# A long convolution with a SwiGLU FFN on one core: taps loaded as rows, the first inverse with a negated basis, another order

## Chip, cores and metric

The kernel runs on one core of a Trainium2 chip. The metric is the device time of one execution in microseconds (us), taken as the median of the runs. Beside it there is one profiled execution, whose trace is read here. Engines are named as the profile names them: PE is TensorE, DVE is VectorE, ACT is ScalarE, POOL is GpSimd, and SP is the engine that issues most DMAs. A label such as L695 is a line of the kernel before.

## The reference, cut to what matters

With S = 2048 rows and D = 640 channels:

```
k_shift = sum over t of pad(k)[:, t:t+S] * shift_k[:, 3-t]     # four taps
kv      = k_shift * v
y       = irfft(rfft(kv, 2S) * rfft(ssm_k, 2S))[:, :S] + kv * ssm_D
h       = x + layernorm(x) * y
out     = h + (silu(n @ w_gate) * (n @ w_up)) @ w_down,  n = layernorm(h)
```

F, the width of the FFN, is 1728. Everything is bf16 in memory.

## The kernel before

The sequence is cut into four blocks of 512 rows; a tile has 128 partitions with four rows r each. Block by block the kernel makes the product kv, its spectrum X, the spectrum G of that block of the filter, the sum of the products of spectra over all earlier blocks, the inverse transform, the gated residual h, the second norm and the FFN.

**Taps (L498 to L506, L885).** The shift convolution is done on PE: `diag` (L885) holds the four taps of each channel on small diagonals, 32 channels wide, and 140 matmuls per block (L504) work on 32-row strips of the transposed k. `tapw`, 128 x 5 x 4, holds the taps channel by channel; it is read straight from memory by L874, where four taps of a channel are 8 bytes in a row. DVE builds `diag` from `tapw` and a folded identity (L882, L883).

**Spectra (`transform`, L324; matmuls L308; evictions L297 on ACT or L300 on DVE).** A spectrum of 512 frequencies is held in two halves. By symmetry the second half needs only another sign of the odd rows, so in the plain form ("sub") the odd part is evicted twice over and DVE subtracts (L343). In the form "four" DVE has six operations in place of that one (L360, L364, L367), and PE half of the matmuls. In the form with `minus`, a second basis that is the negated and scaled one, PE accumulates the second half itself, with six matmuls in place of four per quarter, and DVE has nothing to do. Block 0 works in two pieces of 320 channels (`SPLIT`). G0 takes `minus`; X0 does not.

**Products (`mac`, L531; L538 for the first term, L564 and L565 for the others).** All on DVE.

**Inverse (`inverse`, L646; matmuls L695).** In the plain form DVE first makes the difference and the sum of the two halves (L656, L659), and PE uses four matmuls per row and piece. With `minus` there is no DVE work and there are eight matmuls per row and piece. Then the first norm is applied (L637), the result is multiplied with the inverse (L707), and added to x (L713); ACT sums squares (L577); the small steps of the norm are L590 to L612 on DVE; the second norm is applied by L637 on DVE or L640 on ACT; `turn_h` transposes h on PE (L733) or by DMA and ACT or DVE evict it (L735).

**FFN (`ffn`, L754).** L775 and L810 are gate and up, 512 columns per matmul; L792 is the silu, L799 and L801 the product, or L798 straight from PSUM; L842 is the down projection, 320 columns per matmul; L847 and L848 add the result to the output in memory, and in the last block L857 and L859 with a store by SP (L861).

**The order.** Each step is recorded as a numbered operation with its engine, its reads and its writes (`Plan.add`). `Plan.run` emits them in the order of the table `ORDER`. A negative entry -n stands for operation n - 1 on the other engine that it offers: an eviction that is on ACT goes to DVE, and the product L799 with L801 becomes the one L798. Buffers come from pools of fixed size (`SLOTS`), handed out when an operation first touches them: four PSUM tiles `ps`, twelve large tiles `big`, five `row` tiles. Engines work in their program order, so the table also sets which wait blocks what. On SP, loads that must wait for a buffer hold up the loads behind them.

`DIRECT` names the spectra and the inverse that take `minus`; `SUM` names those that take "four". `ACTLN` and `ACTLN2` say from or in which blocks a norm is offered to ACT. X0 and G0 are given no name at L903 and L904, so that `SUM` isn't looked up for them.

Of the kernel before, what the change touches and what calls it, by code (L numbers as in the profile page):

```python
# [11 lines left out]
BF16 = mybir.dt.bfloat16  # L12
# [7 lines left out]
P = 128  # L20
# [6 lines left out]
KT = D // P  # L27
# [5 lines left out]
ADDLO, ADDMAC, ADDWIN, ADDH, LEAD = (), (), (), (2,), {}  # L33
PAD = 16
WARM = 24
DIRECT, ACTLN, ACTKV, ACTLN2 = ('G0',), 1, 1, (2, 3)
LN1DVE, LN2POOL, HTURN = (0, 1, 2, 3), (), (2, 1)
GTURN = (3, 1, 2)
SUM = {'i3': 'four', 'G1': 'four', 'X1': 'four', 'X0': 'four'}
ADDP = {}  # L40
K0TURN = False
SLOTS = {"S": 8, "big": 12, "kT": 2, "tT": 1, "row": 5, "sg": 2, "ps": 4, "sm": 6}
ORDER = (
# [44 lines left out]
SPLIT = ((0,), (1,))  # L88
ROWS = (1, 3, 0, 2)
HALVES = (ROWS[:2], ROWS[2:])  # L90
# [81 lines left out]
def kernel(ctx: ExitStack, tc: tile.TileContext, A_q, A_k, A_v, A_shift_k, A_ssm_k, A_ssm_D, B_x,  # L172
          B_w_gate, B_w_up, B_w_down, out):
    nc = tc.nc
# [20 lines left out]
    def new(kind):  # L195
        return Buf(views.get(kind, (kind,))[0], kind)

    def fixed(shp, dt, name):
        return Buf(None, None, const.tile(shp, dt, name=name))

    def ap(b):
        if b.pool is None:
            return b.ap
        t = place[b.pool][b.at]
        _, how, sizes = views.get(b.kind, (None, None, None))
        return t.rearrange(how, **sizes) if how else t

    def pe(ns, fn, r, w):
        return plan.add("pe", ns, fn, r, w)
# [12 lines left out]
    def load(nbytes, fn, w, r=()):  # L222
        return plan.add("sp", nbytes / 300.0, fn, r, w)
# [23 lines left out]
    ident = fixed([P, P], BF16, "ident")  # L247
    WF = fixed([P, R, 4, P], BF16, "WF")
    WI = fixed([P, 4, R, P], BF16, "WI")
    tapw = fixed([P, KT, 4], BF16, "tapw")  # L250
    diag = fixed([P, KT * 4, ROWT], BF16, "diag")
    eye = fixed([P, 2 * ROWT], BF16, "eye")
    wd = fixed([P, NCH, D], BF16, "wd")
# [144 lines left out]
    def turned(b):  # L398
        return ap(b).rearrange("p a b -> p (a b)").bitcast(BF16)
# [24 lines left out]
    def spectrum(src, pieces=((0, 1),), minus=None, name=None):  # L424
        b = new("S")
        transform(src, b, pieces, minus, name)
        return Spec(b)
# [443 lines left out]
            nc.gpsimd.memset(t[64:P, NC_FULL, :], 0.0)  # L871
    plan.add("pool", 2000, blank, [], [blanks])
    k = load_k(0)
    load(1e3, lambda: nc.sync.dma_start(out=ap(tapw), in_=A_shift_k.rearrange("(c p) t -> p c t", p=P)), [tapw])  # L874
    idle = new("ps")

    def warm():
        for _ in range(WARM):
            nc.tensor.matmul(ap(idle)[:, 0, 0:P], ap(ident), ap(ident), start=True, stop=True)
    pe(110 * WARM, warm, [ident], [idle])  # L880
    def fold():
        nc.vector.tensor_add(ap(eye), ap(ident)[:, 0:2 * ROWT], ap(ident)[:, 2 * ROWT:P])  # L882
        nc.vector.tensor_add(ap(eye)[:, 0:ROWT], ap(eye)[:, 0:ROWT], ap(eye)[:, ROWT:2 * ROWT])  # L883
# [8 lines left out]
    minus = new("tT")  # L892
# [7 lines left out]
        k = turned_k(k)  # L900
    kv = kv_of(0, k, None, v)
    gT = g_turned(g, drow)
    X = [spectrum(kv, SPLIT, minus if "X0" in DIRECT else None)]  # L903
    G = [spectrum(gT, SPLIT, minus if "G0" in DIRECT else None)]  # L904
    H = [G[0]]
    n1 = ln1(x)
    A = Spec(new("S"))
# [77 lines left out]
```

## Time and profile before

| | us |
|---|---|
| median of three runs | 265.37 |
| lowest and highest | 264.68, 266.27 |
| the profiled execution, its own time | 265.86 |
| its span in the trace | 263.8 |
| PE busy in the span | 247.7 |
| DVE busy | 209.3 |
| ACT busy | 173.4 |
| POOL busy | 22.1 |

The page cuts the span into 40 slices of 6.6 us and gives the busy share of each engine in tenths, with the TensorE clock granted in the row PEclk. A timeline line has start, length, engine, line, operation, tiles and count, and in brackets the idle time before it with what ended it. A line of the waits has who waited for whom, the total in us, the number of times and the longest.

### The profile page before, as it was taken

The page shows a single profiled execution, that of the slowest core. Times are in us where ns is not written, and L with a number is a line of the kernel's source. Part 1 is how long each engine was busy: PE and PEld are TensorE (multiplying, and loading weights), DVE is VectorE, ACT ScalarE, POOL GpSimd, SP SyncE. Part 2 cuts the span into 40 slices and gives each one's busy share as a digit, 9 for nine tenths or more (in the row PEclk, how much of TensorE's full clock was granted, in tenths as well). Part 3 has the DMA queues.
Part 4 walks back from the last instruction along what each step waited for, and adds up shares of the span by engine and source line. Part 5 has one row for each costly group of instructions (what it writes and reads, how often), then busy time and mean ns, then how long its engine had stood idle before and what let it go on. Part 6 is the DMA issues. An engine that isn't in the chain of part 4 may idle for free. (4 is left out here: it accounts for less than half of the span.)

```text
span 263.8 us, 5064 instructions
## 1 busy us (share of the span) xinstructions
PE 247.7 (94%) x2004; PEld 146.1 (55%) x2004; DVE 209.3 (79%) x326; ACT 173.4 (66%) x296; POOL 22.1 (8%) x26
## 2 busy tenths in 40 slices
PE   3989596999999999999999999999999999999995
PEld 3866363544555777754445667544447774444673
DVE  2589989989999999899999999999999831122122
ACT  3799979999888959653538886359743871462200
POOL 2001700000000004010001300220000004000000
PEclk9999779999999999999999999999999999999999
DMA  6889499994687857999389634867999007000011
GB/s 169 311 276 276 110 191 222 316 255 66 159 303 249 143 115 132 116 230 244 93 197 235 98 102 88 162 133 183 283 262 261 3 2 99 0 0 2 0 50 50
DMA packets 73880, 40.81 MB, mean 155 GB/s; under 512 B 34113, under 2 KB 71810, under 8 KB 73858
## 3 DMA queue, kind: packets, MB, share of 16 engines
q1 hardware_dynamic: 71554, 37.88, 56.6%
q0 software_dynamic: 2304, 2.62, 7.7%
q8 instruction: 15, 0.25, 0.4%
q14 instruction: 7, 0.06, 0.1%
HBM read 30.01 MB, written 4.59 MB: 131 GB/s over the span
## 5 line engine op out<-in xcount | busy, mean ns | idle before, releaser
L775 PE MATMUL ps<-big,big 128*128 128x512 bf16 x480 | 106.2, 379 | 0.8 <-ACT sg L792 0.6
L775 PEld LDWEIGHTS <-big 128*128 128x128 bf16 x480 | 46.8, 98 | 56.8 <-issue 1.4
L842 PE MATMUL ps<-wd,tT 128*128 128x320 bf16 x448 | 62.8, 299 | 0.0
L842 PEld LDWEIGHTS <-tT 128*128 128x128 bf16 x448 | 43.8, 98 | 17.3
L792 ACT ACTIVATE sg<-ps 128x1024 bf16<-128x1024 f32 (+1 forms) x28 | 27.0, 965 | 35.5 <-PE ps L775 13.7
L308 PE MATMUL ps<-big,WF 128*128 128x320 bf16 x224 | 35.1, 302 | 3.0 <-ACT S L297 2.1
L564 DVE TENSOR_TENSOR big<-S,S 128x2560 bf16<-128x2560 bf16 x24 | 35.3, 1479 | 0.0
L565 DVE TENSOR_TENSOR S<-S,big 128x2560 bf16<-128x2560 bf16 x24 | 35.2, 1479 | 0.0
L308 PEld LDWEIGHTS <-WF 128*128 128x128 bf16 x224 | 22.0, 99 | 14.0 <-issue 3.7
L799 ACT CAST sg<-ps 128x1024 bf16<-128x1024 f32 (+1 forms) x26 | 24.6, 948 | 4.8 <-PE ps L775 4.5
L801 DVE TENSOR_TENSOR tT<-sg,sg 128x1024 bf16<-128x1024 bf16 (+1 forms) x26 | 16.7, 642 | 10.7 <-ACT sg L799 10.7
L577 ACT ACTIVATE row<-big 128x640 bf16<-128x640 bf16 x32 | 23.5, 738 | 2.0 <-DVE big L713 1.9
L848 POOL DMA_DIRECT2D out_dram<-row x12 | 10.7, 1136 | 144.3 <-ACT row L847 136.3
L297 ACT CAST S<-ps 128x320 bf16<-128x320 f32 (+1 forms) x39 | 19.3, 544 | 4.1 <-PE ps L308 3.9
L640 ACT ACTIVATE row<-big,sm 128x640 bf16<-128x640 bf16 x18 | 15.7, 923 | 4.9 <-DVE sm L590 4.9
L695 PEld LDWEIGHTS <-WI 128*128 128x128 bf16 x112 | 11.6, 104 | 9.8 <-issue 3.9
L810 PE MATMUL ps<-big,big 128*128 128x512 bf16 x60 | 14.4, 379 | 0.0
L297 ACT ACTIVATE big<-ps 128x640 bf16<-128x640 f32 (+1 forms) x23 | 13.6, 636 | 1.2 <-PE ps L308 1.0
L707 DVE SCALAR_TENSOR_TENSOR row<-row,ps 128x640 bf16<-128x640 bf16 x16 | 12.9, 814 | 0.9 <-PE ps L695 0.5
L629 ACT ACTIVATE row<-big 128x640 bf16<-128x640 bf16 x16 | 11.7, 736 | 2.0 <-DMA big<-in_A_q_dram 2.0
L538 DVE TENSOR_TENSOR S<-S,S 128x2560 bf16<-128x2560 bf16 (+1 forms) x10 | 12.1, 1215 | 0.0
L538 DVE TENSOR_TENSOR big<-S,S 128x2560 bf16<-128x2560 bf16 (+1 forms) x10 | 12.1, 1215 | 0.0
(78 smaller groups left out, 233.0 us busy)
## 6 DMA issues: line engine op xcount, KB each, us to landing
big<-in_B_w_up_dram SPq DMA_DIRECT2D x24, 320.0 KB, 4.5
big<-in_B_w_gate_dram SPq DMA_DIRECT2D x24, 320.0 KB, 3.9
big<-in_A_q_dram SPq DMA_DIRECT2D x4, 640.0 KB, 6.3
big<-in_A_v_dram SPq DMA_DIRECT2D x4, 640.0 KB, 4.4
big<-in_A_ssm_k_dram SPq DMA_DIRECT2D x4, 640.0 KB, 7.0
wd<-in_B_w_down_dram SPq DMA_DIRECT2D x1, 2080.0 KB, 10.7
out_dram<-big SPq DMA_DIRECT2D x3, 640.0 KB, 5.4
out_dram<-row POOLq DMA_DIRECT2D x12, 160.0 KB, 4.6
```

The costliest lines, as they stand in the source:

```text
L297: (lambda: nc.scalar.activation(dst(), src(), ACT.Copy, scale=2.0)) if twice else (lambda: nc.scalar.copy(dst(), src())),
L308: nc.tensor.matmul(ap(ps)[:, h, 0:NH], w, ap(src)[:, r, h * NH:(h + 1) * NH], start=(first and i == 0), stop=(last and i == len(rs) - 1), ...
L538: return lambda: f(*(x() for x in args))
L564: dve(1490, lambda b=b, xs=xs, hs=hs: nc.vector.tensor_mul(flat2(b), X.part(xs), H.part(hs)), [X.at(xs), H.at(hs)], [b])
L565: dve(1490, lambda b=b, dst=dst, f=f: f(A.part(dst), A.part(dst), flat2(b)), [b], [A.at(dst)])
L577: act(930, lambda r=r, junk=junk: nc.scalar.activation(ap(junk), ap(x)[:, r, :], ACT.Square, scale=D ** -0.5, accum_out=sm(s, 1)[:, r:r + ...
L640: nc.scalar.activation(ap(row), ap(x)[:, r, :], ACT.Identity, bias=sm(s, 5)[:, r:r + 1], scale=sm(s, 4)[:, r:r + 1])
L775: nc.tensor.matmul(of(ps, i), ap(w)[:, k, off:off + P], ap(hT)[:, k, lo:lo + n], start=(k == 0), stop=(k == KT - 1))
L792: act(1010 if wide else 600, lambda: nc.scalar.activation(of(sg), of(*gate), ACT.Silu), [gate[0]] if gate[0] is up[0] else [(gate[0], gate ...
L799: op = plan.add("act", 1010 if wide else 590, lambda: nc.scalar.copy(of(co), of(*up)), psu + [sg], [co] + tt, ("dve", 1230 if wide else 69 ...
L801: op.rest = dve(690 if wide else 420, lambda: nc.vector.tensor_mul(to(), of(sg), of(co)), [sg, co], tt)
L842: nc.tensor.matmul(ap(to)[:, hf, 0:NH], ap(tT)[:, c, at:at + P], ap(wd)[:, c, hf * NH:(hf + 1) * NH], start=(c == order[0]), stop=(c == or ...
```

## The change

The taps are loaded as five rows of 128 channels by four taps (1 KB each), into a new tile `tap5` on five partitions. PE transposes them, one transpose of 128 x 5 per tap, and one eviction writes `tapw`. The load stands between the two halves of the first k. The inverse of block 0 takes `minus`. The table `ORDER` is another one, with the numbers of the operations moved by two. `ACTLN` and `ACTLN2` now offer more norm steps to ACT, and the table takes the other engine for some; X0 and G0 get their names, and `SUM` loses X0.

```diff
-DIRECT, ACTLN, ACTKV, ACTLN2 = ('G0',), 1, 1, (2, 3)
+DIRECT, ACTLN, ACTKV, ACTLN2 = ('G0', 'inv0'), 0, 1, (0, 1, 2, 3)
-SUM = {'i3': 'four', 'G1': 'four', 'X1': 'four', 'X0': 'four'}
+SUM = {'i3': 'four', 'G1': 'four', 'X1': 'four'}
 ORDER = (
...
+    tap5 = fixed([KT, P * 4], BF16, "tap5")
...
-    load(1e3, lambda: nc.sync.dma_start(out=ap(tapw), in_=A_shift_k.rearrange("(c p) t -> p c t", p=P)), [tapw])
+    load(1e3, lambda: nc.sync.dma_start(out=ap(tap5), in_=A_shift_k.rearrange("(c p) t -> c (p t)", p=P)), [tap5])
...
+    pt = new("ps")
+
+    def turn_taps(pt=pt):
+        for t in range(4):
+            nc.tensor.transpose(turned(pt)[:, t * 8:t * 8 + KT], ap(tap5).rearrange("c (p t) -> c t p", t=4)[:, t, :], ap(ident)[0:KT, 0:KT])
+    pe(240, turn_taps, [tap5, ident], [pt])
+    evict(lambda copy, pt=pt: copy(ap(tapw).rearrange("p c t -> p t c"), turned(pt)[:, 0:32].rearrange("p (t c) -> p t c", c=8)[:, :, 0:KT]),
+          [pt], [tapw], ns=200, other=140)
...
-    X = [spectrum(kv, SPLIT, minus if "X0" in DIRECT else None)]
-    G = [spectrum(gT, SPLIT, minus if "G0" in DIRECT else None)]
+    X = [spectrum(kv, SPLIT, minus if "X0" in DIRECT else None, "X0")]
+    G = [spectrum(gT, SPLIT, minus if "G0" in DIRECT else None, "G0")]
```

Counted over the built programs, PE gains 32 matmuls of L695 and the four transposes. DVE loses two L656 and two L659 of 320 columns by four rows and one eviction of the transposed k, and gains three evictions of spectra (two of 320 columns and one of 640) and one of h. ACT loses those and gains the eviction of k and that of the taps. All other groups keep their counts on each engine.

88 rows, old and new, of the table ORDER are left out of this document.

## The prediction

> **What bounds the kernel now.** I read the page first, for the share of each engine and for the stretches in which the busiest one is not busy.
>
> ```profile
> PE 247.7 (94%) x2004; PEld 146.1 (55%) x2004; DVE 209.3 (79%) x326; ACT 173.4 (66%) x296; POOL 22.1 (8%) x26
> PE   3989596999999999999999999999999999999995
> DVE  2589989989999999899999999999999831122122
> PEclk9999779999999999999999999999999999999999
> ```
>
> TensorE (PE) is the bound over the whole span, and VectorE (DVE) runs beside it without a hole up to the thirtieth slice, about 198 us. So two chains are nearly equally late. Only the front is loose: slices 5 to 8 of the PE row hold 5, 9, 6, and in two of them the granted clock is 0.7. The waits of PE say what ended those holes:
>
> ```profile
> PE ps L695 <- ACT big L524: 2.9, 1, 2.9
> PE ps L308 <- ACT S L297: 2.1, 4, 0.9
> ```
>
> The timeline of PE places them, and gives the point at which the first FFN begins:
>
> ```profile
> 14.90 4.55 PE L308 MATMUL ps<-big,WF 128*128 128x320 bf16 x32 [0.71 <-ACT big L393]
> 26.19 1.43 PE L504 MATMUL ps<-diag,kT 32*128 32x128 bf16 x140
> 30.50 1.23 PE L695 MATMUL ps<-big,WI 128*128 128x320 bf16 x4 [2.88 <-ACT big L524]
> 34.04 2.34 PE L695 MATMUL ps<-S,WI 128*128 128x320 bf16 x8
> 48.22 4.49 PE L775 MATMUL ps<-big,big 128*128 128x512 bf16 x20
> ```
>
> And the chain that ended last gives the rest (start, length, what):
>
> ```profile
> 142.89 1.42 DVE big L528
> 168.64 6.47 PE ps L775 x30
> 197.77 5.43 PE ps L842 x40
> 260.67 0.49 DVE row L859
> ```
>
> From 144.3 us, when DVE finishes the product L528 of the last block, the chain is PE alone up to the last DVE addition. Its rates are prices: 6.47/30 = 0.216 us for a 512-wide matmul, 5.43/40 = 0.136 for a 320-wide one. In the instruction order of the two built programs the PE work from the first L775 on is equal in both: 540 of 512, 648 of 320 columns and the same small ones, 208.7 us at these rates. So the change is worth what it moves the first L775 (48.22) and the L528 of the last block (144.3), plus new waits behind them.
>
> **The taps.** Three windows of 1 us and two for the clock (the last columns are granted clock, DMA share, GB/s):
>
> ```profile
> 4.00:5.00 1.00, 1.00 (x11) 1.00 (x11) 0.36 (x1) 0.00 (x0) 0.00 (x0) 1.00 0.98 101
> 5.00:6.00 1.00, 1.00 (x12) 0.93 (x9) 0.48 (x4) 0.83 (x2) 0.00 (x0) 1.00 0.97 215
> 8.00:9.00 1.00, 1.00 (x63) 0.88 (x52) 0.00 (x0) 0.59 (x1) 0.00 (x0) 1.00 1.01 391
> 29.00:30.00 1.00, 0.00 (x0) 0.00 (x0) 1.00 (x2) 1.00 (x3) 1.00 (x1) 0.78 0.00 0
> 36.00:37.00 1.00, 1.00 (x8) 0.64 (x7) 0.58 (x1) 0.24 (x1) 0.00 (x0) 0.81 1.32 291
> ```
>
> Between 4 and 6 us the DMA engines are fully busy and move 101 and 215 GB/s, against 391 later: this is where 640 runs of 8 bytes pass. Five rows of 1 KB should give back at most (1 - 101/391) + (1 - 215/391) = 1.2 us to whatever stands behind them in the queue, at least nothing. Behind them stand x and v, and both are waited for:
>
> ```profile
> 5.92 0.82 DVE L885 TENSOR_TENSOR diag<-eye,tapw 128x640 bf16<-128x640 bf16 x1 [0.49 <-DMA tapw<-in_A_shift_k_dram]
> 10.11 2.48 DVE L526 TENSOR_TENSOR big<-ps,big 128x512 bf16<-128x512 f32 x4 [2.96 <-DMA big<-in_A_v_dram]
> 20.60 0.82 DVE L538 TENSOR_TENSOR big<-S,S 128x1280 bf16<-128x1280 bf16 x1
> 25.76 0.81 DVE L656 TENSOR_TENSOR big<-S 128x1280 bf16<-128x1280 bf16 x1
> 26.49 0.82 DVE L538 TENSOR_TENSOR S<-S,S 128x1280 bf16<-128x1280 bf16 x1
> 31.82 1.55 DVE L659 TENSOR_TENSOR S<-S 128x1280 bf16<-128x1280 bf16 x2
> 39.67 0.81 DVE L707 SCALAR_TENSOR_TENSOR row<-row,ps 128x640 bf16<-128x640 bf16 x1
> 44.14 1.51 DVE L637 TENSOR_SCALAR row<-big,sm 128x640 bf16<-128x640 bf16 x4
> 201.38 1.56 DVE L673 TENSOR_TENSOR S<-S 128x1280 bf16<-128x1280 bf16 x2
> ```
>
> ScalarE (ACT), which sits in the turn of G0 and in the eviction of every spectrum, shows the same wait for x and then hardly any:
>
> ```profile
> 8.41 0.74 ACT L629 ACTIVATE row<-big 128x640 bf16<-128x640 bf16 x1 [1.95 <-DMA big<-in_A_q_dram]
> 23.15 3.62 ACT L297 CAST S<-ps 128x320 bf16<-128x320 f32 x10 [0.16 <-PE ps L308]
> 29.09 2.61 ACT L524 CAST big<-ps 128x512 bf16<-128x512 f32 x6
> 31.52 2.59 ACT L378 COPY big<-big 128x2560 bf16<-128x2560 bf16 x1
> 36.76 1.29 ACT L297 CAST S<-ps 128x640 bf16<-128x640 f32 x2 [1.44 <-PE ps L308]
> 41.25 0.76 ACT L577 ACTIVATE row<-big 128x640 bf16<-128x640 bf16 x1
> 46.78 1.29 ACT L735 COPY big<-ps 128x640 bf16<-128x640 bf16 x2
> ```
>
> Against this gain: diag now waits for four transposes of 5 columns and a small copy. No row shows such a copy; it lies between nothing and the 0.65 us of one of the L524 or kT copies (1.29 for two in the L735 row), and I take 0.3, as it moves 20 of 640 columns. It stands on ACT behind two kT copies, so diag starts near 6.1 instead of 5.92 and the last kT copy, now behind diag on DVE, ends about 0.3 later than before. The kT transposes and taps on PE run that much later, under the wait for v (10.11), then the warm-up block, the rest of the taps and the turn of G0 follow without a hole. So the spectra (L308) start at about 14.2 instead of 14.90: PE's own queue keeps 0.7 of the 1.2. Bounds: from 0.3 later to 1.2 earlier. On SP a transposing load of the next k now stands ahead of the 1.2 KB row of D and of WI and the basis; it is issued once the kT transposes are done, some 5 us sooner than before, behind everything the front waits for, and I cost it at nothing. If the row of D were late, G0's turn would wait for it.
>
> **The inverse of block 0.** Removed from DVE: four operations of 320 columns by four rows (two L656, two L659). Start to start such an operation takes 0.74 (25.76 to 26.49), so 2.95 us. Added on PE: 32 matmuls of 0.136, 4.35 us. Further moves in the order up to the end of the first h: ACT gives two 320-wide and one 640-wide eviction to DVE (0.4 each; 0.8), three L637 go behind the products, and one difference L360 (0.4) goes behind the norm. Step by step:
>
> The spectra end, and the taps of the next block begin, at 25.5 (26.19 less 0.7); the last eviction ends at about 25.95 (23.15 + 3.62 = 26.8, less 0.8, as ACT has two fewer of them). DVE has the products of piece 0 done by then, so piece 1 starts at 25.95 instead of 26.49 and, with L656 no longer among its neighbours, A is complete at 25.95 + 6 x 0.74 = 30.4. Before, the low rows were ready at 33.4 (31.82 + 1.55). That is 3 us, but PE must use them: it does taps until 26.9, eight and eight matmuls of piece 0 until 29.1, waits to 30.4, then 24 matmuls (33.7), four L308, eight, four, eight, two, eight: the last inverse row is ready at 38.4, and its L707 starts at 38.55 instead of 39.67. The intermediate L707, L713 and the kv product (1.5, behind L524) on DVE end by 38.3, so PE sets it. Then ACT's last square sum starts at 40.0 instead of 41.25, and the norm, without the L360 inside it, is followed by the four L637, which end at 44.05 instead of 45.65: **1.6 us earlier**. ACT evicts 13 L297 and 4 L577 from 34.1 on; at 0.59 and 0.73 start to start that is 10.6 us, so the two L735 end at 46.0 instead of 48.07, and the first L775 starts at 46.1, **2.1 us earlier**.
>
> The added 4.35 us of PE thus go into the hole of 2.88 and the stretch where the clock was halved: between the last matmul of L504 (27.6) and 36 us, 320-wide matmuls took 2.34/8 = 0.29. If that cover is gone they cost up to 4.35.
>
> **What is late next.** From the end of those L637 to the last block's L528 DVE has 0.4 us less work in the new order (one L707 fewer, one L360 more):
>
> ```profile
> L360 DVE TENSOR_TENSOR S<-S 128x640 bf16<-128x640 bf16 x4 | 1.9, 483 | 0.0
> L707 DVE SCALAR_TENSOR_TENSOR row<-row,ps 128x640 bf16<-128x640 bf16 x16 | 12.9, 814 | 0.9 <-PE ps L695 0.5 <-issue 0.3
> ```
>
> So L528 ends 2.0 earlier, and PE comes 2.1 earlier: they still meet. But from there to the last inverse DVE has that L707 and one small operation more, 0.9 us, while PE has the same. Before, the two met closely there: L673 ends at 201.38 + 1.56 = 202.9 and PE ends its 40 L842 at 203.2. I take a new wait of 0.8 on PE (bounds 0 and 0.9); nothing but L842 and L695 in fixed order is queued behind it. All later PE work is the same; the last group still ends in one 320-wide L859 and an 80 KB store, 0. The rest of the edits do nothing: L637 and L640 keep their counts of 14 and 18, and X0 had no name before, so its 'four' was never used.
>
> **The sum.** - 2.0 + 0.8 = -1.2 us against the profiled execution (265.86 us, a span of 263.8 and 2.06 around it), which is 0.49 above the median 265.37 of the runs. Against the median: **264.2 us**. Bounds: with the taps' 0.3 later to 1.2 earlier the front gives 1.0 to 2.5 in place of 2.0; the last wait costs 0 to 0.9.
>
> **Rivals.**
> 1. *The halved clock stays, slower.* A mean of 0.78 from 29 to 30 us is half speed for the last 0.44, so the clock fell near 29.56, 1.9 us after the last matmul ended at 27.62; by the 0.81 from 36 to 37 it came back near 36.4. In the new order PE is idle from 29.1 to 30.4, 1.3 us, after a dense 2.2 us. If an idle stretch of that size is enough, or A comes 0.6 us later so that it reaches 1.9, the matmuls between 30.4 and 36.4 run at half speed with twice as many L695 to do: 3.0 us lost. The last L707 then starts at 41.55, the L637 end at 47.05 (+1.4), and with -0.4 and +0.8 behind it the time is 1.8 above before, 267.2. For it: the fall in the row. Against it: the four waits for L297, of at most 0.9, in slices at full clock. Chance 0.20.
> 2. *The short rows buy nothing.* If x and v land as late as before and only the longer way to diag counts, the spectra start at 15.0: 0.8 of the gain goes, 265.0. For it: the copy of v has k, x and itself to move at any rate. Chance 0.17.
> 3. *No new wait at the last inverse.* DVE and PE keep their 2.0: 263.4. For it is one wait of DVE, from 48 to 66 us, that may go because ACT reaches the first gate sooner by as much as DVE, but DVE has an L360 more to do ahead of it; it would pay for the new wait.
>
> ```profile
> DVE tT L801 <- ACT sg L799: 0.8, 1, 0.8
> ```
>
> Chance 0.13.
> 4. *The forecast*, 263.2 to 265.0: 0.50.
>
> [...]
>
> **How the numbers follow.** A measurement of this kernel tells about 0.5%, 1.3 us, from no change; the forecast lies just inside. Faster by more: half of the forecast's chance and a little (0.27) and rival 3 (0.13), 0.40. Within: the rest of the forecast (0.23) and most of rival 2 (0.12), 0.35. Slower by more: rival 1 (0.20) and the tail of rival 2 with a worse front (0.05), 0.25. The range goes from the best front with no wait behind it and without the 0.8 of DVE, 265.37 - 2.5 - 0.8 = 262.1, to rival 1, 267.2.
>
> **What would show it.** Right: tapw's small copy and diag near 6, L526 before 9.5, L308 at 14.2; a clock row without a 7 and a hole of about 1.3 us ahead of piece 1 of L695; the first L775 near 46; L528 of the last block near 142.3; a new wait of PE for L673 near 201. Wrong: a 7 left in the clock row, L526 still at 10.1, or PE waits of over 1 us anywhere between 50 and 200.

## The result, and the profile after

| | before | after |
|---|---|---|
| median of 17 runs each, us | 265.37 | 263.95 |
| lowest and highest | 263.93, 267.05 | 262.64, 264.93 |
| the profiled execution | 265.86 | 263.05 |
| its span | 263.8 | 261.4 |

The ratio is 0.9946 with a 95% interval of 0.9924 to 0.9969: the change saves 1.4 us (0.8 to 2.0). The profiled pair differs by 2.8 us, twice as much, so its stages show where time went but not how much of it is typical. Of the runs of the kernel before that stand beside the experiments, one took 434.61 us at a granted clock of 0.568; it is left out below. Lines of after are those of before plus one in the range that matters (L308 is L309, L504 is L505, L695 is L696, L775 is L776).

The page of after, the rows of PE, of DVE and of the granted clock:

```profile
PE 249.5 (95%) x2040; PEld 148.1 (57%) x2040; DVE 207.8 (79%) x325; ACT 172.9 (66%) x294; POOL 18.3 (7%) x26
PE   3989997999999999999999999999999999999995
DVE  1579999999999999999999999999999831122132
PEclk9999999999999999999999999999999999999999
```

The two 7s of the clock row are gone, and of the loose slices 5 to 8 one 7 is left. The timeline of PE, the steps that the prediction priced:

```profile
15.45 1.83 PE L309 MATMUL ps<-big,WF 128*128 128x320 bf16 x12 [0.82 <-ACT big L394]
26.53 1.80 PE L505 MATMUL ps<-diag,kT 32*128 32x128 bf16 x140
28.26 1.80 PE L696 MATMUL ps<-S,WI 128*128 128x320 bf16 x12
31.03 0.70 PE L696 MATMUL ps<-S,WI 128*128 128x320 bf16 x4 [0.42 <-DVE S L539]
46.95 1.24 PE L776 MATMUL ps<-big,big 128*128 128x512 bf16 x5
200.53 1.25 PE L696 MATMUL ps<-S,WI 128*128 128x320 bf16 x8
```

The spectra run on without a break 0.55 us **later** than before (15.45 against 14.90). The hole ahead of the inverse is 0.42 us in place of 2.88, the clock stays full (a mean of 0.999), and the first FFN starts 1.27 us earlier (46.95 against 48.22). DVE's last product:

```profile
139.73 1.48 DVE L529 TENSOR_TENSOR big<-big,big 128x2560 bf16<-128x2560 bf16 x1
```

It ends at 141.2, 3.1 us earlier than before. The last inverse row is at 200.53 with no wait ahead of it. ACT, DVE and the windows show the front (last columns: clock, DMA share, GB/s):

```profile
8.95 0.74 ACT L630 ACTIVATE row<-big 128x640 bf16<-128x640 bf16 x1 [1.57 <-DMA big<-in_A_q_dram]
14.72 1.26 ACT L394 COPY big<-ps 128x640 bf16<-128x640 bf16 x2
10.60 3.15 DVE L527 TENSOR_TENSOR big<-ps,big 128x512 bf16<-128x512 f32 x6 [2.88 <-DMA big<-in_A_v_dram]
```

```profile
4.00:5.00 1.00, 0.93 (x9) 0.93 (x10) 0.00 (x0) 0.18 (x1) 0.00 (x0) 1.00 0.75 264
5.00:6.00 1.00, 0.60 (x8) 0.32 (x7) 0.00 (x0) 1.00 (x3) 0.00 (x0) 1.00 1.01 315
8.00:9.00 1.00, 1.00 (x80) 1.00 (x71) 0.00 (x0) 0.05 (x1) 0.12 (x1) 1.00 0.94 290
```

From 4 to 6 us more bytes move than before (264 and 315 GB/s against 101 and 215), yet x (8.95) and v (10.60) are there 0.5 us later.

### The profile page after: what moved, and what is told of

Read it like the earlier page. It is cut to its first block, busy times and chain, and to the rows that moved or that the text cites. A ratio compares the mean times of both kernels' runs of the same rounds, so it can differ in the third digit from the quotient of the medians.

```text
span 261.4 us, 5121 instructions
## 1 busy us (share of the span) xinstructions
PE 249.5 (95%) x2040; PEld 148.1 (57%) x2040; DVE 207.8 (79%) x325; ACT 172.9 (66%) x294; POOL 18.3 (7%) x26
## 4 chain that ended last, share of the span: by engine, by line
PE 72%; DVE 14%; ACT 7%; DMA 3%; issue 2%; SPq 0%; ACTq 0%
PE ps L776 32%; PE ps L843 22%; PE ps L309 9%; PE ps L696 4%; PE ps L811 4%; DMA big<-in_A_q_dram 3%; DVE S L539 2%; ACT S L298 2%; DVE S L566 2%; DVE big L565 2%; ACT row L578 2%; DVE big L539 2%; DVE tT L802 1%; ACT row L630 1%; DVE S L437 1%
## 5 line engine op out<-in xcount | busy, mean ns | idle before, releaser
L776 PE MATMUL ps<-big,big 128*128 128x512 bf16 x480 | 105.8, 379 | 0.3 <-ACT sg L820 0.2
L776 PEld LDWEIGHTS <-big 128*128 128x128 bf16 x480 | 46.8, 98 | 56.1 <-issue 1.1
L843 PE MATMUL ps<-wd,tT 128*128 128x320 bf16 x448 | 63.5, 299 | 0.0
L309 PE MATMUL ps<-big,WF 128*128 128x320 bf16 x224 | 35.6, 299 | 1.9 <-ACT big L394 0.8
L309 PEld LDWEIGHTS <-WF 128*128 128x128 bf16 x224 | 21.8, 97 | 13.2 <-issue 3.3
L298 ACT CAST S<-ps 128x320 bf16<-128x320 f32 (+1 forms) x36 | 18.0, 547 | 3.8 <-PE ps L309 3.4
L696 PEld LDWEIGHTS <-WI 128*128 128x128 bf16 x128 | 12.4, 98 | 6.0 <-issue 1.1
L696 PE MATMUL ps<-S,WI 128*128 128x320 bf16 x96 | 15.0, 299 | 0.4 <-DVE S L539 0.4
```

Of the source, the lines that this page charges most:

```text
L298: (lambda: nc.scalar.activation(dst(), src(), ACT.Copy, scale=2.0)) if twice else (lambda: nc.scalar.copy(dst(), src())),
L309: nc.tensor.matmul(ap(ps)[:, h, 0:NH], w, ap(src)[:, r, h * NH:(h + 1) * NH], start=(first and i == 0), stop=(last and i == len(rs) - 1), ...
L696: nc.tensor.matmul(ap(ps)[:, w, 0:NH], m, src[:, w * NH:(w + 1) * NH], start=(i == 0), stop=(i == len(terms) - 1))
L776: nc.tensor.matmul(of(ps, i), ap(w)[:, k, off:off + P], ap(hT)[:, k, lo:lo + n], start=(k == 0), stop=(k == KT - 1))
L843: nc.tensor.matmul(ap(to)[:, hf, 0:NH], ap(tT)[:, c, at:at + P], ap(wd)[:, c, hf * NH:(hf + 1) * NH], start=(c == order[0]), stop=(c == or ...
```

## The experiments

Theory A: the gain is block 0's inverse (2.95 us off DVE, its PE work in the hole). Theory B: the short rows. Theory C: the order table alone. Theory D came up on the way: the gain is the clock that no longer falls. Each time below is a median with its ratio to the kernel before, run on the same chip.

**1. After with the old taps load, at the new place.**

```diff
-    load(... in_=A_shift_k.rearrange("(c p) t -> c (p t)", p=P)), [tap5])
+    load(... in_=A_shift_k.rearrange("(c p) t -> p c t", p=P)), [tapw])
-    pe(240, turn_taps, ...); evict(...)
```

> The kernel after, with the taps loaded as before (640 runs of 8 bytes, no transposes, no small copy), at the same place between the halves of k; everything else as after. Theory A (the gain is that of block 0's inverse and of the order around it, the short rows are worth nothing): x is waited for until about 8.4 us and v until 10.1 as in the kernel before, the first L775 (here without the five new lines) comes 0 to 0.5 us earlier than in after (46.95), and the time is that of after, 263.95, or up to 0.5 below: 263.4 to 264.0. Theory B (the short rows give the gain): back to the time before, 265.0 to 265.4. Theory C (the order behind block 0 gives it): as after, 263.9.

Measured: 262.93, ratio 0.9901 (0.9870 to 0.9932). Theory B falls: without the short rows the kernel is no slower. The time is 0.5 below the range that theory A gave. Its spectra, a line of the timeline of PE (here L310):

```profile
14.48 2.78 PE L310 MATMUL ps<-big,WF 128*128 128x320 bf16 x18 [0.46 <-ACT big L395]
```

**2. Before with the negated basis in block 0's inverse, nothing else.**

```diff
-DIRECT, ... = ('G0',), ...
+DIRECT, ... = ('G0', 'inv0'), ...
```

> The kernel before with one thing changed: block 0's inverse takes the negated basis (no L656 and L659 in block 0, eight L695 per row and piece), all the rest in the order of before. Theory A in its narrow form (taking 2.95 us from DVE is enough): the first L775 comes 1 us or more earlier than 48.22 and the time is 264.0 to 264.5. Rival A2 (the hole of 2.88 us is not set by DVE but by PSUM, which L524 frees behind a 2.6 us copy L378 on ACT; so the order must change with the inverse): the hole and the halved clock stay, the 32 added matmuls run at half speed (0.29 in place of 0.136 each), the first L775 comes later than 48.22 and the time is 266 to 270. Theory C: 265.4, no change.

Measured: 268.40, ratio 1.0115 (1.0079 to 1.0152): 3 us slower. Rival A2's price holds. The timeline of PE and two windows:

```profile
27.94 1.43 PE L504 MATMUL ps<-diag,kT 32*128 32x128 bf16 x140
32.25 0.70 PE L695 MATMUL ps<-S,WI 128*128 128x320 bf16 x4 [2.88 <-ACT big L524]
```

```profile
13.00:14.00 1.00, 0.08 (x1) 0.09 (x2) 0.71 (x4) 1.00 (x4) 0.00 (x0) 0.97 0.13 40
17.00:18.00 1.00, 1.00 (x8) 0.63 (x6) 0.42 (x4) 0.90 (x3) 0.00 (x0) 0.82 1.05 392
31.00:32.00 1.00, 0.00 (x0) 0.00 (x0) 1.00 (x2) 1.00 (x3) 0.00 (x0) 1.00 0.46 151
```

The hole is 2.88 us to the hundredth as before, though DVE's work ahead of it is less: the inverse waits for a PSUM tile that L524 frees, and L524 stands on ACT behind the 2.6 us copy L378. So 32 more matmuls, 4.35 us at 0.136, stand behind the same hole. Yet in this profile the clock did not fall in that hole (1.00); it fell at 13.94, in the front, and came back at 17.36. So in this profile that half of A2 (these matmuls at half speed) did not come. The profiled run is the only one of the six at a granted clock of 0.993; the other five have 0.987, and no trace shows where theirs fell.

**3. After with the transposing load of the next k behind the row of D and WI.**

```diff
-ORDER: 14, 13, 191, 16, 17, 15, 193
+ORDER: 14, 13, 16, 191, 17, 15, 193
```

> The kernel after with one DMA issue moved: the transposing load of the next k's first row stands behind the row of D and WI, as in before, and not ahead of them. In after it was issued at 7.22 us and x and v landed 0.5 us later than in before. If that load is what delays them, x is there at 8.4 and v at 10.1, and the time is 0.2 to 0.6 below after, 263.4 to 263.7. If it is the five rows or the halves of k, x stays at 8.95 and v at 10.6, and the time is 263.95.

Measured: 264.16, ratio 0.9944 (0.9922 to 0.9966), as after. x came at 8.64 and v at 10.34 in its profile, halfway between the two expectations, which tells nothing; by the time, the early load costs nothing that can be seen.

**4. Before with idle matmuls in the hole.**

```diff
+            if blk == 1 and len(cs) == 1:
+                for _ in range(14):
+                    nc.tensor.matmul(ap(banks[1])[:, 1, 128:448], ap(WF)[:, 0, 0, :], <320 columns of WF>)
```

> The kernel before with 14 idle 320-wide matmuls (1.9 us, into unused columns of a PSUM tile) behind the taps of block 1, where PE stood idle for 2.88 us; they compute nothing that is read. It tests what the halved clock alone cost. If the clock fell because of that hole and the inverse of block 0 was held up by it: no 7 is left in the clock row, the 28 L695 up to 36 us take 0.136 in place of 0.29 each, and the first L775 comes 0.5 to 1.5 us earlier than 48.22; time 264.0 to 264.9. If DVE (its L656, L659 and L707) sets the end of block 0 all the same: the clock is full and the first L775 stays at 48.2, time 265.4. If the idle matmuls only delay L524's release of PSUM: up to 1.9 later, 267.

Measured: 264.02, ratio 0.9951 (0.9920 to 0.9982). **Work that computes nothing gives the kernel before as much as the change does, as far as these intervals tell.** Each run lists its granted clock, and the twelve runs fall in two groups: five at 1.0 with a median of 263.26 (263.01 to 264.04), seven at 0.991 to 0.994 with 265.09 (263.45 to 265.47). PE and its windows in the profiled one (0.994):

```profile
28.99 2.08 PE L510 MATMUL ps<-WF 128*128 128x320 bf16 x14
31.99 0.70 PE L700 MATMUL ps<-big,WI 128*128 128x320 bf16 x4 [0.92 <-ACT big L529]
48.43 1.90 PE L780 MATMUL ps<-big,big 128*128 128x512 bf16 x8
```

```profile
14.00:15.00 1.00, 0.29 (x3) 0.12 (x2) 0.83 (x3) 1.00 (x4) 0.00 (x0) 0.84 0.78 106
18.00:19.00 1.00, 1.00 (x9) 0.69 (x8) 0.90 (x6) 0.80 (x3) 0.00 (x0) 0.95 1.18 243
29.00:30.00 1.00, 1.00 (x16) 0.73 (x9) 1.00 (x2) 1.00 (x1) 0.00 (x0) 1.00 0.08 16
```

At 29 us the clock is full, as meant; but it fell once in the front, from 14.68 to 18.10, where the expectation had no loss at all. In this execution, one of those at 0.994, the first FFN (L780) starts at 48.43, no earlier than before (48.22): the expected 0.5 to 1.5 us do not show in it. They show in the profile of experiment 10, at a full clock.

**5. The old load behind both halves of k, else after.** The edit is that of experiment 1, with 5 behind 4 in the order.

> The kernel after with the old taps load (640 runs of 8 bytes), now behind both halves of k as in the kernel before; the only difference to the run that had the old load between the halves (262.93) is this place. If the old form as such is the better one (no transposes, no small copy, no PSUM tile), the time stays at 262.9 (262.6 to 263.3). If it is the place between the halves that helped (there the 8-byte runs passed between 3 and 4 us, and the windows from 4 to 6 us moved 333 and 356 GB/s in place of 101 and 215), x is back at 8.3 to 9.0 us and the time at 263.6 to 264.0.

Measured: 263.49, ratio 0.9939 (0.9915 to 0.9963), between the two expectations; x came at 8.49.

**6. The five rows behind both halves of k, else after** (5 behind 4 in the order).

> The kernel after with the five-row load behind both halves of k. If the new form costs because it delays the second half of k (waited for until 5.94 in after), k is complete earlier but the taps are later: diag 0.3 to 0.6 later than 6.26, time 263.9 to 264.4. If the place between the halves is what costs x and v their 0.5 us: x at 8.4, time 263.3 to 263.7. In either case it stays above the old form between the halves, 262.93.

Measured: 262.72, ratio 0.9918 (0.9891 to 0.9946), lower than every expectation; x came at 8.66 and v at 10.35. Old against new is 0.9901 against 0.9946 between the halves, 0.9939 against 0.9918 behind them: the sign turns with the place. One pair does differ: experiments 1 and 3, on one chip, with the old and the new load between the halves, do not overlap (262.48 to 263.28 and 263.37 to 264.72). But experiments 5 and 6, also on one chip, lean the other way and overlap, so no effect of the form or of the place holds over all these runs.

**7. After with the plain inverse of block 0.**

```diff
-DIRECT, ... = ('G0', 'inv0'), ...
+DIRECT, ... = ('G0',), ...
+ORDER: the two L656 and L659 of a piece right behind its products
```

> The kernel after with the plain inverse of block 0 again: DVE has its four L656 and L659 back (2.95 us), each pair right behind the products of its piece, PE has 32 L695 fewer. The order is else that of after. Theory A (the inverse with the negated basis is what the order lives from): A's rows are ready 1.5 us or more later, a hole of 1.5 to 3 us opens ahead of L695, the first L775 comes 1 to 2.5 us later than 46.95, and the time is 265.0 to 266.5. Theory C (the order alone carries the gain, the inverse is neutral): 263.7 to 264.2.

Measured: 266.16, ratio 1.0035 (1.0009 to 1.0060), 2.2 us above after. Theory C falls: the order needs the inverse as the inverse (experiment 2) needs the order. PE and two windows:

```profile
33.21 0.70 PE L697 MATMUL ps<-big,WI 128*128 128x320 bf16 x4 [3.93 <-DVE big L658]
50.38 1.89 PE L777 MATMUL ps<-big,big 128*128 128x512 bf16 x7
```

```profile
34.00:35.00 1.00, 1.00 (x7) 0.65 (x5) 1.00 (x4) 0.91 (x1) 0.00 (x0) 0.63 0.78 161
41.00:42.00 1.00, 1.00 (x7) 0.60 (x6) 0.83 (x3) 0.50 (x1) 0.00 (x0) 0.95 0.24 36
```

A hole of 3.93 us, then half a clock from 34.26 to 41.10, and the first FFN 3.4 us later than in after. Nine of the twelve runs have a granted clock of 0.986 to 0.987, the profiled one, with 6.84 us at half a clock, among them, so the 2.2 us may be the clock's alone: this run does not tell theory A from D.

**8. Experiment 2 with the PSUM wait taken away.**

```diff
-PE:  taps of four groups, taps of the fifth;  ACT: L378, six L524
+PE:  taps of the fifth, taps of four groups;  ACT: two L524 of the fifth, L378, four L524
```

> The kernel before with the negated basis in block 0's inverse, as in the run that took 268.40, and a second edit: of block 1's taps the 28 matmuls of the fifth channel group come first on PE and their two evictions (L524, 128x256) stand ahead of the copy L378 on ACT, as in after, so that two PSUM tiles are free for the first inverse rows. Theory A2 (the hole ahead of L695 was a wait for PSUM behind L378): the 2.88 us wait for L524 goes, the clock stays full, and the time falls from 268.4 to 264.5 to 266. If the hole is the products' (DVE), the wait only changes its name to DVE S L538 and stays above 1.5 us, and the time stays above 267.

Measured: 271.01, ratio 1.0191 (1.0141 to 1.0241); its six runs spread from 268.16 to 273.06. The wait for L524 is gone, as A2 has it, but the time did not fall: the two runs at a clock of 0.993 and 0.994 took 268.2, as in experiment 2, and the four at 0.981 to 0.986 took 270.5 to 273.1. PE and its windows in the profiled run, the longest of the six:

```profile
36.92 1.25 PE L308 MATMUL ps<-big,WF 128*128 128x320 bf16 x4 [3.21 <-DMA big<-big]
37.96 4.47 PE L695 MATMUL ps<-S,WI 128*128 128x320 bf16 x16
```

```profile
15.00:16.00 1.00, 0.69 (x4) 0.45 (x4) 0.91 (x4) 0.99 (x3) 0.00 (x0) 0.77 0.87 115
18.00:19.00 1.00, 1.00 (x5) 0.59 (x4) 0.83 (x7) 0.85 (x2) 0.00 (x0) 0.53 1.03 343
36.00:37.00 1.00, 0.08 (x1) 0.08 (x2) 0.06 (x1) 0.18 (x1) 0.00 (x0) 0.51 0.93 114
42.00:43.00 1.00, 1.00 (x6) 0.60 (x5) 0.53 (x1) 0.00 (x0) 0.00 (x0) 0.58 2.50 96
```

L378 now comes later, with it the DMA transposes of its result, and the order of before has PE do spectra of the next block (L308) ahead of the remaining inverse rows. They wait 3.21 us, the clock falls, and 16 matmuls take 4.47 us. In after these rows stand ahead of that L308.

**9. Experiment 7 with 40 idle matmuls, meant for its hole.**

```diff
+                    if fill:        # block 0, row 1, first piece
+                        for _ in range(40): nc.tensor.matmul(ap(ps)[:, 0, 320:512], ..., <192 columns>)
```

> The kernel after with the plain inverse of block 0, as in the run that took 266.16 (clock 0.987 in nearly all executions, a hole of 3.93 us ahead of L695, first L775 at 50.38), and 40 idle 192-wide matmuls (some 3.3 us at full clock, into unused columns of a PSUM tile, nothing reads them) in that hole. Theory D (the inverse's gain is the clock that it keeps up, by work in the hole): the granted clock is 1.0, the first L775 comes near 47.5 to 48.5 and the time falls to 263.7 to 264.5, about that of after. Theory A (the 2.95 us of DVE are the gain, the clock is a side effect): A's rows are ready no sooner, DVE's end of block 0 stays late, and the time stays at 265.3 or above although the clock is full.

Measured: 269.57, ratio 1.0159 (1.0118 to 1.0201). This tells A and D apart no further: the order issues that row behind the hole, not ahead of it.

```profile
33.81 1.22 PE L698 MATMUL ps<-big,WI 128*128 128x320 bf16 x4 [3.93 <-DVE big L659]
40.58 3.46 PE L701 MATMUL ps<-WF 128*128 128x192 bf16 x40
```

What it does show is a price: 3.46 us of PE work at 40 us, outside any hole, made the kernel 3.4 us slower (269.57 against 266.16). In this place, outside a hole, PE work was paid in full.

**10. Experiment 4 with a longer warm-up block in the front** (`WARM` 36 in place of 24).

> The kernel before with the 14 idle matmuls in block 1's taps, as in the run of 264.02 (263.26 where the granted clock was 1.0, 265.09 where it was 0.994 because it fell once near 14.7 us), and the warm-up block L879 lengthened from 24 to 36 matmuls of 128, 0.7 us at full clock, in the hole of 1.5 us ahead of the last taps. If the fall near 14.7 comes of that hole, nearly all executions show a clock of 1.0 and the median is 263.0 to 263.6: the kernel before with nothing but idle matmuls is then level with after. If the longer block costs more than it keeps (where it runs at half speed it is 1.3 us longer and ends behind v), 264.3 to 265.5.

Measured: 264.41, ratio 0.9977 (0.9949 to 1.0004). The clock is 0.998 or more in 11 of 12 runs, so the fall near 14.7 was that hole's. But the time is not the expected 263.0 to 263.6, and its interval includes no change: the 0.7 us of the longer block may have taken what the clock gave, which no run shows apart. In its profile, at a clock of 1.0, the first FFN starts 1.6 us earlier than before and 0.4 earlier than in after, with idle matmuls alone (0.4 of it is an earlier front, with the spectra at 14.51):

```profile
46.59 4.49 PE L780 MATMUL ps<-big,big 128*128 128x512 bf16 x19
```

**11 and 12. Two of x's eight statistics on DVE, old and new taps behind both halves of k.**

```diff
+            if vec and r < 2:
+                dve(900, lambda ...: nc.vector.scalar_tensor_tensor(ap(junk), ap(x)[:, r, :], 1.0 / D, ap(x)[:, r, :],
+                    op0=ALU.mult, op1=ALU.mult, accum_out=sm(s, 1)[:, r:r + 1]), ...)
```

> A version meant to beat both: the kernel after with the old taps load behind both halves of k (263.49), and two of the eight statistics of x (L577, two square sums) on DVE instead of ACT, in the time in which DVE waits for v. In the kernels before and after, ACT does eight in a row from the landing of x to the evictions of G0's turn (L393), for which PE waits 0.4 to 0.9 us. If ACT is what holds the spectra up, that wait goes, the spectra start 0.4 to 0.7 us sooner than 14.56, and the time is 262.8 to 263.1. If v or WF is as late, nothing is won: 263.4; if the two operations delay the product with v on DVE: 263.6 to 264.

> The same with the five rows of taps behind both halves of k (262.72 without the statistics moved): 262.1 to 262.5 if ACT holds the spectra up, 262.7 if not. Beside the run with the old load it also compares the two forms of the taps once more at the same place in one call: if the form is worth nothing that can be told, the two lie within 0.7 us.

Measured: 262.62, ratio 0.9901 (0.9864 to 0.9938), and 262.96, ratio 0.9913 (0.9886 to 0.9941). The timeline of PE of the first:

```profile
12.29 1.37 PE L393 MATMUL ps<-ident,big 128*128 128x128 bf16 x20
13.62 3.56 PE L310 MATMUL ps<-big,WF 128*128 128x320 bf16 x24
```

No wait is left ahead of the spectra and they start at 13.62, as DVE does the two sums between 8.23 and 9.8, where it waited for v. But this does not show that ACT held them up in experiment 5. There, and in experiment 12, PE waited for the load of the basis WF (the timelines of PE, experiment 5 first):

```profile
14.56 2.67 PE L310 MATMUL ps<-big,WF 128*128 128x320 bf16 x17 [0.77 <-DMA WF<-const_wf]
14.45 2.62 PE L310 MATMUL ps<-big,WF 128*128 128x320 bf16 x18 [0.48 <-DMA WF<-const_wf]
```

So the 0.9 us between experiments 11 and 5 (263.49) can be WF's earlier landing as well as the two sums, and with the new load nothing was won over experiment 6. Against the kernel before beside it (265.37), 262.62 is the fastest median here, 1.0% below by the ratio; that it beats experiments 1, 6 and 12, these intervals cannot tell.

## Why the prediction was right in the sum, and where its steps failed

The forecast was 264.2 and the median is 263.95; the sign and size of the sum held. Its steps did so only in part.

**The bound held.** PE is the chain from the first FFN on, and what the change is worth is decided ahead of it. All of the 2.4 us of span are there when DVE ends its last product (3.1) and PE its last inverse row (200.53 against 203.04, 2.5).

**The taps failed, in the step "the spectra (L308) start at about 14.2 instead of 14.90".** They ran from 15.45. Two things were missed. First, the bound of "0.3 later to 1.2 earlier" took one profile's landing times for fixed. Five profiles have the same loads as before (before itself and experiments 2, 4, 8 and 10): x is there at 8.41, 8.99, 8.27, 8.83 and 7.38, v at 10.11, 10.67, 9.98, 10.48 and 9.59. The scatter is as large as the term. Second, the row quoted in the prediction, PE's 0.71 us for L393, was read as PE's own queue; but ACT does eight statistics of x ahead of L393, 5.8 us from x's landing, so in the profiles of before and after x, not v, sets the spectra. Close behind stands the load of WF, which the prediction did not name: in the profiles of experiments 3, 5, 9, 10 and 12 it is what PE waited for last, by 0.48 to 1.20 us. Which of the two an earlier landing of the taps could have moved stays open. The small copy took 0.23 us where 0.3 was priced. Rival 2's step came about, not its time.

**The inverse: right that its work must go into the hole, wrong on what that saves.** The last L707 was forecast at 38.55 and came at 39.10, the norm's end at 44.05 and came at 44.6, the first L775 at 46.1 and came at 46.95: 0.55 to 0.85 late, with A complete at 31.0 instead of 30.4. The hole was 0.42 and not 1.3, because PE's spectra and taps came over 1 us later than forecast (the taps of the next block at 26.53 instead of 25.5) and A only 0.6. What the prediction priced as DVE time is better told as clock. Over the 67 runs of the kernel before that stand beside the experiments, 40 have a granted clock of 0.992 to 0.994 and a median of 264.75, 20 have 0.986 to 0.987 and 265.73, and 7 have 0.978 to 0.981 and 266.82: each step costs about 1.0 us, and none is at 1.0, where this line, drawn on, would give 263.75. All 17 runs of after have 0.998 or more, and take 263.95. Theory D is thus large enough for the whole gain, and experiment 4 shows it from the other side: at a clock of 1.0 its runs (263.26) are level with after. The price of a step is not the same everywhere: in experiment 4 it was 1.8 us (265.09 against 263.26). And experiments 1, 5, 6, 11 and 12, with the new inverse and a full clock, lie 0.3 to 1.1 us below that line, which theory D does not explain. That the inverse is worth nothing beyond the clock is only argued from this: the run that was to show it (9) missed the hole.

**Rival 1, the halved clock, did not come, but its reason was sound.** Half a clock appears as soon as one half of the change stands alone: for 6.84 us in experiment 7, for 3.41 and 6.82 in 8. The step that failed is the one that took the length of the hole for the condition. The same hole of 2.88 us came with a fall in before, 1.94 us after it opened (27.62 to 29.56), and with none in experiment 2, where PE stood idle from 29.37 to 32.25 at a granted clock of 1.00. The clock's falls last 6.83 us in before (29.56 to 36.39), 3.42 in experiments 2 and 4, 6.84 in 7; in 8 they begin at 15.54 and 36.02, 20.48 apart, and end at 18.95 and 42.84; in between the clock reads 0.50. So in these five profiles each fall lasts once or twice 3.41 to 3.42 us, and the two of experiment 8 begin six times that apart. What sets off a fall was not shown: in experiment 4 the clock fell at 14.68, and in the 3.4 us ahead of it PE stood idle for only 1.3, between transposes of 128 columns and 32-row taps.

**The new wait at the last inverse did not come** (rival 3's step): it was worked out from PE and DVE both coming 2.0 us earlier, with 0.9 more of DVE work behind. In the profile DVE came 3.1 earlier and had that 0.9 to spare. One part of the 1.1 between shows in the timeline of DVE, whose wait for the first gate was 0.80:

```profile
53.95 0.69 DVE L802 TENSOR_TENSOR tT<-sg,sg 128x1024 bf16<-128x1024 bf16 x1 [0.47 <-ACT sg L800]
```

From the first FFN to the last inverse row PE stood idle for 1.69 us in before and 0.86 in after (48.22 to 203.04 and 46.95 to 200.53); 0.6 of the difference is the one wait of L775 for L792, which is gone, and 0.2 that of L695 for L656. So the sum was luck: the front gained 1.3 us where 2.1 were forecast, and the 0.8 that was to be lost at the end was not. Another 1.2 us was gained in between; as the profiled pair is twice as far apart as the medians, how much of each is typical stays open.

## What to carry to other kernels

Ahead of pricing an engine's work, look whether the clock row has a dip and what the dip costs in all runs: filling a hole of PE, even with idle matmuls, was worth as much here as the whole change (0.9951 against 0.9946). An edit that shortens one engine's chain pays only if the order lets the next engine use it: the same inverse cost 3 us in the old order and its absence 2.2 in the new one. Before pricing an earlier landing, compare several profiles with the same loads, and look in each at what the waiting engine waited for last: here it was ACT in some and WF in others.

## What was not expected of the hardware

The granted clock of the runs of the kernel before comes in steps of about 0.0065 (0.994, 0.987, 0.981), which is one half of 3.42 us in 264, and in the five profiles with a fall the two agree: 0.987 with 6.83 us of falls in before, 0.993 with 3.42 in experiment 2, 0.994 with 3.42 in 4, 0.987 with 6.84 in 7, 0.981 with 10.23 in 8. The same program is one, two or three such steps below 1 from run to run (40, 20 and 7 of the 67 runs of the kernel before), and two thirds of the variance of their times (263.33 to 267.49) goes with that number. Why the same hole of 2.88 us came with a fall in before and with none in experiment 2 was not shown, and no run was made for it.
